# Writing the second half of a hidden tile behind an older chunk's matmuls, in a fused attention and expert kernel

## The chip, the cores and the metric

The kernel runs on one core of a Trainium2 chip. The metric is device microseconds of one execution; the time of a kernel is the median of its runs. The engines are named as in the profile: PE is TensorE (PEld its weight loads, which can run beside a matmul), DVE is VectorE, ACT is ScalarE, POOL is GpSimd, and SP issues the DMAs.

## The reference

```python
B, N, m, C = (4, 12480, 32, 128)
def mab(q, kv):
    s = scale * (q @ kv.transpose(0, 2, 1))
    a = np.exp(s - s.max(-1, keepdims=True))
    a /= a.sum(-1, keepdims=True) + 1e-09
    return a @ kv
h = mab(I, x)              # 32 inducing points look at all tokens
x = mab(x, h)              # each token looks at the 32 results
h = x @ w_in               # 49920 x 128 @ 128 x 2048
g = h * (1.0 / (1.0 + np.exp(-1.702 * h)))
out = g @ w_out            # 49920 x 2048 @ 2048 x 128
```

The four batches are 49,920 tokens in all. (The reference reuses the name `h`; the shortened lines above do too.)

## The kernel before, in words

The expert layer is nearly all of the work. Tokens go through it in blocks of 512 (96 whole blocks and 2 of 384 left over, `work`, lines 659 to 680). The hidden width of 2048 is cut into 16 chunks of 128, and two chunks make a group, so a block is 8 groups (`NG`) and the whole kernel has 784.

What is done for a group is in two functions.

`first(i)` (line 684) takes one PSUM tile `ph` of 128 x 2 x 512 from a pool of two (`ps_h`, line 98) and writes its two halves with one matmul each (line 693): the stacked attention weights `st` times `hw`, which is the second attention's values already multiplied by `w_in`. Then ScalarE reads both halves in one instruction and writes `g`, the activated values in fp32 (line 701). `hi`, the values rounded for the fast fp32 matmul, is made either by ScalarE from `ph` once more (line 705) or by DVE from `g` (line 707); `lo = g - hi` is made by DVE (line 708). Which engine makes `hi` is decided while the program is written out, by meters that add up an estimated cost for each instruction of ScalarE, DVE and TensorE (`Meter`, line 35; `act.t`, `dve.t`, `pe_.t` at lines 702 to 704). A `ph` tile is free again when ScalarE has read it for the last time.

`second(i, c)` (line 711) multiplies chunk `c` of group `i` by its part of `w_out` and adds it to the block's output in PSUM with three matmuls (`hi` by `wl`, `lo` by `wh`, `hi` by `wh`, lines 720 to 722). With the block's last chunk, ScalarE copies the output to SBUF (line 725) and the DMA to the output is put on a list, `stores`.

The order of all engines is written out by hand (`manual_schedule`, line 102), by the loop at lines 784 to 816. Each turn calls `first(i)`, puts the group's two chunks at the end of the list `under_way`, and then calls `second` for the oldest chunks until only `lag` are left (line 805). So in an ordinary turn TensorE gets two first products, side by side, and then six matmuls of two older chunks. `lag` starts at 6 chunks and grows by one every third turn up to 12 (`LAG`, `EXTRA`, line 813); a turn after which it has just grown leaves one chunk more in the list. The attention of the next batch is written in small steps behind each turn by the generator `rest` (line 809). When that generator yields `LUMP`, it has just put several exponentials into ScalarE's queue; then six older chunks are multiplied at once and `lag` falls back to 6 (lines 810 to 812). The list `stores` is issued on SP at the end of a turn (line 808), and `part`, a step of preparing `hw` for the next batch, is finished right behind `first(i)` (line 796).

Of the kernel before, what the change touches and what calls it, by code (L numbers as in the profile page):

```python
# [55 lines left out]
def set_attention_then_moe(ctx: ExitStack, tc, xT, x, indT, w_in, w_out, outT):  # L56
# [463 lines left out]
    def h_w_in(b, c):  # L520

        if b == 0:
            if c % 2 == 0:
                first_h.append(ps_h.tile([P, 2, 512], F32, tag="ph", name="ph"))
            pa = first_h[-1][:, c % 2]
        else:
            pa = ps_a.tile([P, 512], F32, tag="pa", name="pa")
        pe_.matmul(pa, hTs[b], w_in_sb[:, c * 512:(c + 1) * 512], start=True, stop=True)
        yield
        t = phw.tile([P, 512], F32R, tag="hw", name="hw")  # L530
        act.copy(t, pa)
        dve.tensor_sub(t[P // 2:P], pa[P // 2:P], t[P // 2:P].bitcast(F32))
        hw[b, c] = t
# [46 lines left out]
    def run(gen):  # L580
        for _ in gen:
            pass
# [101 lines left out]
    def first(i):  # L684
        bi, k = divmod(i, NG)
        key, of = work[bi]
        st = stacks[key]
        n = sum(p[2] for p in of)
        ph = ps_h.tile([P, 2, 512], F32, tag="ph", name="ph")
        for c in range(2):  # L690
            ch = 2 * k + c
            for b, at, w, _ in of:
                pe_.matmul(
                    ph[:, c, at:at + w], hw[b, ch // 4][:, ch % 4 * P:(ch % 4 + 1) * P],
                    st[:, at:at + w], start=True, stop=True,
                )
        hi = ph_.tile([P, 2, TOK], F32R, tag="hi", name="hi")
        lo = ph_.tile([P, 2, TOK], F32R, tag="lo", name="lo")
        g = pg.tile([P, 2, TOK], F32, tag="g", name="g")
        ph, hi, lo, g = ph[:, :, 0:n], hi[:, :, 0:n], lo[:, :, 0:n], g[:, :, 0:n]  # L700
        act.activation(g, ph, AF.Gelu_apprx_sigmoid)
        act.t = max(act.t, pe_.t)
        dve.t = max(dve.t, pe_.t)
        if act.t + 70 + 1.667 * n <= dve.t + 70 + 1.04 * n:
            act.activation(hi, ph, AF.Gelu_apprx_sigmoid)
        else:
            dve.tensor_copy(hi, g)
        dve.tensor_sub(lo, g, hi.bitcast(F32))
        parts[i] = hi, lo

    def second(i, c):
        bi, k = divmod(i, NG)
        key, of = work[bi]
        n = sum(p[2] for p in of)
        ch = 2 * k + c
        if ch == 0:
            outs[bi] = ps_o.tile([P, 512], F32, tag="po", name="pso")
        o = outs[bi][:, 0:n]
        hi, lo = parts.pop(i) if c else parts[i]
        pe_.matmul(o, wl[:, ch, :], hi[:, c, :], start=(ch == 0), stop=False)  # L720
        pe_.matmul(o, wh[:, ch, :], lo[:, c, :], start=False, stop=False)
        pe_.matmul(o, wh[:, ch, :], hi[:, c, :], start=False, stop=(ch == NCH - 1))
        if ch == NCH - 1:
            ob = po.tile([P, TOK], F32, tag="ob", name="ob")
            act.copy(ob[:, 0:n], o)
            for b, at, w, t0 in of:
                stores.append((i + 3, outT[:, t0:t0 + w], ob[:, at:at + w]))
            outs.pop(bi)
# [39 lines left out]
    under_way = []  # L768
# [7 lines left out]
    def lay_out():  # L776

        key = turns.pop(0)
        while key not in es:
            next(rest)  # L780
        return weights_of(*key), key

    i, lag, last = 0, LAG[0], 0
    while i < n or under_way:
        now[0] = i
        if i < n:
            if back is None and turns and i >= begin[turns[0]]:
                back, laid = lay_out()
            while back is not None and first_block[laid] * NG <= i:
                run(back)  # L790
                back = None
                if turns and first_block[turns[0]] * NG <= i:
                    back, laid = lay_out()
            first(i)
            if part is not None:
                run(part)
                part = None
            if products and products[0][0] == i:
                part = h_w_in(*products.pop(0)[1:])
                next(part)  # L800
            under_way += [(i, 0), (i, 1)]
            i += 1
        else:
            lag = 0
        while len(under_way) > lag:
            second(*under_way.pop(0))
        while stores and (stores[0][0] <= i or not under_way):
            nc.sync.dma_start(*stores.pop(0)[1:])
        if i < n and next(rest, None) is LUMP:
            while len(under_way) > LAG[0]:  # L810
                second(*under_way.pop(0))
            lag, last = LAG[0], i
        if lag < LAG[1] and i - last >= EXTRA:
            lag, last = lag + 1, i
        if back is not None and next(back, 0) == 0:
            back = None
# [33 lines left out]
```

## Time and profile before

| what | value |
|---|---|
| median of 3 runs | 1630.17 us (1630.16 to 1631.4) |
| the profiled execution's own time | 1632.7 us |
| its span, first to last instruction | 1630.9 us |
| mean granted clock of TensorE | 0.992 |
| first products (`ph<-st,hw`, 512 columns) | 1536, 401 ns each in the profile |
| matmuls into the output (`pso`, 512 columns) | 3 x 1536, 394 to 399 ns each |
| ACT `g<-ph` | 784, mean 1030 ns |
| ACT `hi<-ph` | 464, mean 1022 ns |
| DVE `hi<-g` | 320, mean 749 ns |
| DVE `lo<-g,hi` | 784, mean 1268 ns |
| ACT `ob<-pso` | 98, mean 591 ns |

A matmul's time in the profile includes its way through the array, which overlaps the next one; the distance between starts is what counts, not the duration. In a timeline a row gives the start, the duration, the engine, the line (46 for nearly all, a helper's), the operation, the tiles written and read, and how many instructions in a row were merged into it; in brackets stand the idle time of the engine ahead of it and what ended it. In the list of waits a row gives who waited, for whom, the total in us, the number of times and the longest. Releasers are inferred; "issue" means that the profile shows none.

### The profile page before, as it was taken

The numbers are of one execution on the slowest core, as the hardware profiler recorded it, in microseconds if no ns is written. First come the engines' busy times: TensorE is split into PE (matmuls) and PEld (weight loads), VectorE is DVE, ScalarE is ACT, GpSimd is POOL, SyncE is SP. The second block draws the span as 40 slices with busy tenths as digits, with TensorE's granted clock in tenths as the row PEclk, the third lists the DMA queues.
The fourth block names the chain that finished last, engine by engine and source line by source line (L and its number), as shares of the span: only waits on it lengthen the run. The fifth ranks groups of instructions, "written<-read, shape, count | busy, mean of one in ns | idle before, by whom it ended". The sixth has DMA issues, their size and how long they took to land.

```text
span 1630.9 us, 21863 instructions
## 1 busy us (share of the span) xinstructions
PE 1591.0 (98%) x7737; PEld 1233.0 (76%) x7737; DVE 1386.9 (85%) x1515; ACT 1331.5 (82%) x1513; POOL 197.9 (12%) x134
## 2 busy tenths in 40 slices
PE   6799999999999999999999999999999999999999
PEld 3477777787777877777766877777777888888887
DVE  7788978988889887888888988878988888889886
ACT  5488888888878878987888878988788888888885
POOL 4311100103101011011120110110121101101100
PEclk9899999999999999999999999999999999999999
DMA  8304219503042112850205101671301011011010
GB/s 338 104 16 175 64 37 203 120 19 97 19 142 76 43 39 56 184 126 20 91 14 202 40 27 39 136 183 40 97 16 42 25 39 46 20 39 46 22 44 20
DMA packets 81947, 126.66 MB, mean 78 GB/s; under 512 B 11632, under 2 KB 50096, under 8 KB 75696
## 3 DMA queue, kind: packets, MB, share of 16 engines
q1 hardware_dynamic: 81840, 125.26, 27.1%
q8 instruction: 63, 1.03, 0.3%
q14 instruction: 44, 0.36, 0.1%
HBM read 74.10 MB, written 25.56 MB: 61 GB/s over the span
## 4 chain that ended last, share of the span: by engine, by line
PE 88%; DVE 4%; ACT 3%; DMA 2%; issue 2%; SPq 1%; POOL 0%; ACTq 0%; DVEq 0%; POOLq 0%
PE pso L46 62%; PE ph L46 22%; PE pa L46 4%; DMA xt<-in_xT 2%; DVE lo L46 2%; ACT g L46 1%; ACT hi L46 1%; SPq L575 1%; DVE sm L46 1%; DVE hi L46 0%; DVE e L46 0%; DVE m L46 0%; DVE hw L46 0%; DVE t L46 0%; ACT s L46 0%
## 5 line engine op out<-in xcount | busy, mean ns | idle before, releaser
L46 DVE TENSOR_TENSOR lo<-g,hi 128x1024 fp32r<-128x1024 f32 (+1 forms) x784 | 983.1, 1268 | 134.4 <-ACT hi L46 122.0
L46 ACT ACTIVATE g<-ph 128x1024 f32<-128x1024 f32 (+1 forms) x784 | 804.3, 1030 | 232.2 <-PE ph L46 119.0
L46 PE MATMUL pso<-hi,wl 128*128 128x512 f32 (+1 forms) x1568 | 623.7, 398 | 0.0
L46 PE MATMUL pso<-hi,wh 128*128 128x512 f32 (+1 forms) x1568 | 617.3, 394 | 0.0
L46 PE MATMUL pso<-lo,wh 128*128 128x512 f32 (+1 forms) x1568 | 616.6, 393 | 0.0
L46 PE MATMUL ph<-st,hw 128*128 128x512 f32 x1536 | 491.2, 401 | 6.8 <-ACT hi L46 2.7
L46 ACT ACTIVATE hi<-ph 128x1024 fp32r<-128x1024 f32 (+1 forms) x464 | 474.1, 1022 | 0.0
L46 PEld LDWEIGHTS ph<-st,hw 128*128 128x128 f32 x1536 | 282.2, 188 | 100.5 <-issue 18.7
L46 PEld LDWEIGHTS pso<-lo,wh 128*128 128x128 f32 x1568 | 294.5, 188 | 73.2 <-issue 2.2
L46 PEld LDWEIGHTS pso<-hi,wl 128*128 128x128 f32 x1568 | 295.3, 188 | 70.4 <-issue 2.9
L46 PEld LDWEIGHTS pso<-hi,wh 128*128 128x128 f32 x1568 | 294.9, 188 | 70.3
L46 DVE CAST hi<-g 128x1024 fp32r<-128x1024 f32 x320 | 239.6, 749 | 77.0 <-ACT g L46 76.7
L547 POOL TENSOR_TENSOR e<-e,sm 128x512 f32<-128x512 f32 (+1 forms) x27 | 44.0, 1631 | 1132.8 <-DVE sm L46 1132.8
L46 ACT COPY ob<-pso 128x512 f32<-128x512 f32 (+1 forms) x98 | 58.0, 591 | 17.5 <-PE pso L46 17.5
L474 POOL TENSOR_TENSOR e<-e,m 128x512 f32<-128x512 f32 (+1 forms) x27 | 42.5, 1574 | 180.4 <-DVE m L46 135.8
L551 POOL TENSOR_TENSOR e<-e,ah 128x512 f32<-128x512 f32 (+1 forms) x27 | 49.5, 1834 | 2.2
L46 PE MATMUL pa<-xt,indT_sb 128*32 128x512 f32 x192 | 27.6, 676 | 17.2 <-DMA xt<-in_xT 17.2
L46 ACT ACT_TABLE_LOAD x28 | 35.9, 1283 | 9.8 <-issue 6.3
L550 POOL CAST ah<-e 128x512 fp32r<-128x512 f32 (+1 forms) x27 | 30.3, 1122 | 1.7
L46 PEld LDWEIGHTS pa<-xt,indT_sb 128*32 128x32 f32 x192 | 4.8, 114 | 28.7 <-issue 15.6
L46 PE MATMUL pa<-xt,hT 128*32 128x512 f32 x192 | 25.5, 637 | 1.0 <-DVE hT L46 1.0
L46 ACT ACTIVATE e<-e 128x512 f32<-128x512 f32 (+1 forms) x28 | 14.2, 572 | 9.5 <-DVE e L46 7.6
(97 smaller groups left out, 452.9 us busy)
## 6 DMA issues: line engine op xcount, KB each, us to landing
xt<-in_xT SPq DMA_DIRECT2D x48, 1024.0 KB, 7.1
out_T<-ob SPq DMA_DIRECT2D x96, 256.0 KB, 2.0
xn<-in_x SPq DMA_DIRECT2D x72, 256.0 KB, 6.8
st<-ahT SPq DMA_DIRECT2D x192, 64.0 KB, 2.0
st<-alT SPq DMA_DIRECT2D x192, 64.0 KB, 2.0
raw<-in_w_in SPq DMA_DIRECT2D x4, 512.0 KB, 8.6
raw<-in_w_out SPq DMA_DIRECT2D x4, 512.0 KB, 7.1
xt_last<-in_xT SPq DMA_DIRECT2D x4, 96.0 KB, 8.2
```

The source lines that it names most:

```text
L46: return f(*a, **k)
L474: eng.tensor_sub(e[0:q], e[0:q], m2[0:q, 0:k].unsqueeze(2).broadcast_to([q, k, M]))
L547: eng.tensor_mul(e[0:q], e[0:q], sm[0:q, 0:nb].unsqueeze(2).broadcast_to([q, nb, M]))
L550: eng.tensor_copy(ah[0:q, 0:w], e2[0:q])
L551: eng.tensor_sub(e2[0:q], e2[0:q], ah[0:q, 0:w].bitcast(F32))
L575: nc.sync.dma_start(st[32 * r:32 * r + 32, at:at + w].bitcast(F32), src[32 * j:32 * j + 32, 0:w])
```

## The change

`first` becomes a generator that stops once, between its two chunks. The loop writes the first chunk's product, then one older chunk's three matmuls if the list would be over `lag` with one more chunk in it, and then the rest of `first`: the second chunk's product, and all instructions of ScalarE and DVE. The number of older chunks multiplied in each turn does not change; one of them stands between the two products.

```diff
@@ -694,6 +694,8 @@
                     ph[:, c, at:at + w], hw[b, ch // 4][:, ch % 4 * P:(ch % 4 + 1) * P],
                     st[:, at:at + w], start=True, stop=True,
                 )
+            if c == 0:
+                yield
         hi = ph_.tile([P, 2, TOK], F32R, tag="hi", name="hi")
         lo = ph_.tile([P, 2, TOK], F32R, tag="lo", name="lo")
         g = pg.tile([P, 2, TOK], F32, tag="g", name="g")
@@ -791,7 +793,11 @@
                 back = None
                 if turns and first_block[turns[0]] * NG <= i:
                     back, laid = lay_out()
-            first(i)
+            begun = first(i)
+            next(begun)
+            if len(under_way) + 1 > lag:
+                second(*under_way.pop(0))
+            run(begun)
             if part is not None:
                 run(part)
                 part = None
```

## The prediction

> **What bounds the kernel now.** I read the page first: the span, the busy shares, and the chain that ended last.
>
> ```profile
> span 1630.9 us, 21863 instructions
> PE 1591.0 (98%) x7737; PEld 1233.0 (76%) x7737; DVE 1386.9 (85%) x1515; ACT 1331.5 (82%) x1513; POOL 197.9 (12%) x134
> PE 88%; DVE 4%; ACT 3%; DMA 2%; issue 2%; SPq 1%; POOL 0%; ACTq 0%; DVEq 0%; POOLq 0%
> ```
>
> TensorE sets the end. What it does not spend multiplying it spends waiting, and the change adds and removes no matmul. So the question is which waits of TensorE it makes or takes away. Next I read the groups by line, for what stands between a first product and the reuse of its PSUM tile, and the waits of TensorE's weight loads, since the semaphore wait of a first product sits on its load.
>
> ```profile
> L46 ACT ACTIVATE g<-ph 128x1024 f32<-128x1024 f32 (+1 forms) x784 | 804.3, 1030 | 232.2 <-PE ph L46 119.0 <-ACT g L46 81.7 <-DVE lo L46 16.2
> L46 ACT ACTIVATE hi<-ph 128x1024 fp32r<-128x1024 f32 (+1 forms) x464 | 474.1, 1022 | 0.0
> L46 ACT COPY ob<-pso 128x512 f32<-128x512 f32 (+1 forms) x98 | 58.0, 591 | 17.5 <-PE pso L46 17.5
> PEld ph L46 <- issue: 25.8, 46, 1.7
> PEld ph L46 <- ACT hi L46: 12.8, 25, 1.5
> PEld ph L46 <- ACT g L46: 4.5, 9, 1.7
> ```
>
> There are 784 groups. In 464 of them ScalarE reads the tile ph twice (g, then hi, about 1.95 us together, since the second starts 0.1 us before the first has ended), in the other 320 once. There are two ph tiles, so the first product of group i+2 waits until ScalarE has finished with group i. Today those waits are small: 43.1 us in 80 places, beside 784 groups. How much room is behind them is read from the timelines of an ordinary stretch: first TensorE, then ScalarE, then one weight load.
>
> ```profile
> 1458.27 0.63 PE L46 MATMUL ph<-st,hw 128*128 128x512 f32 x2
> 1460.14 0.63 PE L46 MATMUL ph<-st,hw 128*128 128x512 f32 x2
> 1463.87 0.39 PE L46 MATMUL ph<-st,hw 128*128 128x512 f32 x1
> ...
> 1460.85 1.03 ACT L46 ACTIVATE g<-ph 128x1024 f32<-128x1024 f32 x1 [0.87 <-ACT g L46]
> 1461.77 1.02 ACT L46 ACTIVATE hi<-ph 128x1024 fp32r<-128x1024 f32 x1
> ...
> 1463.64 0.42 PEld L46 LDWEIGHTS ph<-st,hw 128*128 128x128 f32 x2
> ```
>
> A group of eight matmuls takes 1460.14 - 1458.27 = 1.87 us, 0.233 us each. The pair of 1460.14 ends at 1460.77; g begins 0.08 later, hi ends at 1462.79, and the load that needs the tile starts at 1463.64: 0.85 us of room. ScalarE had been idle before that g, so here TensorE, not ScalarE, sets when the tile comes free.
>
> **The change part by part.** *The move in an ordinary group.* Three products of an older chunk go between the pair. ScalarE reads both halves at once, so g waits for the later one: 3 x 0.233 = 0.70 us later, while the first product of group i+2 is not later at all. The room falls from 0.85 to 0.15 us; a load can start 0.05 us after a release, so nothing waits. Cost: nothing, with 0.10 us of cover left. Where ScalarE is behind and g starts late anyway, the move is hidden by that lateness.
>
> *Groups with one chunk fewer.* The lag grows by one every third group from 6 to 12, after the start and after each of 13 lumps (four in each of three attentions, one in the first): 14 x 6 = 84 groups after which only one older chunk is multiplied. Before and after the change such a group has its pair side by side (the new condition is false in it), but the group ahead of it is split, and the load two groups on comes 0.70 us earlier than usual. One of them, in the timelines of TensorE, ScalarE and the loads:
>
> ```profile
> 1094.33 0.63 PE L46 MATMUL ph<-st,hw 128*128 128x512 f32 x2
> 1096.19 0.63 PE L46 MATMUL ph<-st,hw 128*128 128x512 f32 x2
> 1097.34 0.63 PE L46 MATMUL ph<-st,hw 128*128 128x512 f32 x2
> ...
> 1095.00 1.02 ACT L46 ACTIVATE g<-ph 128x1024 f32<-128x1024 f32 x1
> 1095.92 1.02 ACT L46 ACTIVATE hi<-ph 128x1024 fp32r<-128x1024 f32 x1
> ...
> 1097.11 0.42 PEld L46 LDWEIGHTS ph<-st,hw 128*128 128x128 f32 x2
> ```
>
> From 1096.19 to 1097.34 is only 1.15 us. hi of the group ahead ends at 1096.94 and the load starts at 1097.11: 0.17 us of room. With g 0.70 us later hi ends at 1097.64, and the load starts at 1097.69, 0.58 us late.
>
> What a late load costs is read from three pairs: one whose load had to wait a little, one where it waited long, and (above) 0.63 us for an undisturbed pair.
>
> ```profile
> 97.77 0.31 PEld L46 LDWEIGHTS ph<-st,hw 128*128 128x128 f32 x2 [0.15 <-ACT hi L46]
> 97.89 0.63 PE L46 MATMUL ph<-st,hw 128*128 128x512 f32 x2
> ...
> 1265.38 0.30 PEld L46 LDWEIGHTS ph<-st,hw 128*128 128x128 f32 x2 [0.30 <-ACT hi L46]
> 1265.38 0.73 PE L46 MATMUL ph<-st,hw 128*128 128x512 f32 x2
> ```
>
> A load normally leads its product by 0.23 us (1097.11 to 1097.34). At 97.77 the lead had shrunk to 0.12 and the pair still took 0.63. At 1265.38 it was gone and the pair took 0.73, since the next load was late too. So a load that is x late costs x - 0.23 + 0.10 = x - 0.13 us: for 0.58, 0.45 us. Where g starts 0.08 instead of 0.04 us behind its product (the two values above), it is 0.50.
>
> Going through the 84 in the timelines, 33 are of this kind: ScalarE makes hi of the group ahead, it is not already late, and no attention matmul stands in between. The first is the one at 97.77, the last the one at 1265.38. I take 0.48 for each: 33 x 0.48 = 15.8 us. In the others DVE makes hi (41% of groups), attention work delays the load, or ScalarE is late already. Bounds: if the 464/784 = 59% of hi groups held for all 84 with no shared cover, 50 x (0.58 + 0.10) = 34 us; the lower one is with the rivals.
>
> *Smaller losses behind these.* In 29 other places the room left now is below 0.70 us, because ScalarE has an output copy, an exponential or a table load in its queue, and there the delay comes through in part. The first and the last:
>
> ```profile
> 147.01 1.95 ACT L46 ACTIVATE g<-ph 128x1024 f32<-128x1024 f32 x2
> 148.51 0.42 PEld L46 LDWEIGHTS ph<-st,hw 128*128 128x128 f32 x2
> ...
> 1271.67 1.02 ACT L46 ACTIVATE hi<-ph 128x1024 fp32r<-128x1024 f32 x1
> 1273.24 0.42 PEld L46 LDWEIGHTS ph<-st,hw 128*128 128x128 f32 x2
> ```
>
> The load of 1273.24 has 0.55 us of room (hi ended at 1272.69), so it would be 0.20 late and cost 0.07 to 0.12; that of 148.51 has 0.47 (the first g ends at 148.04) and costs 0.14. At 0.15 each the 29 make 4.4 us. Bounds: 0 (TensorE, once delayed, leaves ScalarE time to catch up) and twice that.
>
> *The older chunk's other instructions.* An output copy follows the chunk that completes a block. While the lag is odd (9 groups in each of 14 ramps, 126 of 784, so 16 of the 98 copies) the completing chunk is the one moved, and its copy now stands ahead of g in ScalarE's queue. It can start when its product ends, 3 x 0.233 + 0.40 = 1.10 us after the group's start, takes 0.59, and g could start at about 1.38: 0.31 us late, behind 0.10 + 0.13 of cover where hi follows on ScalarE. 16 x 0.1, about 1 us; bounds 0 and 5. Its DMA to the output is only appended to a list at that point and is issued on SP at the end of the turn as before. Nothing is moved past another transfer or past POOL's queue.
>
> *The older products themselves.* The first of them needs hi and lo one matmul after the group's start, not two, and lo is up to 0.70 us later. DVE's lo is normally several groups ahead (the lag is 6 to 12 chunks, 3 to 6 groups of 1.87 us), except for the groups right behind a lump; 0 to 3 us, taken as none beyond what TensorE's own new waits cover.
>
> *The planner.* `first` reads TensorE's meter three products later, which raises ScalarE's and DVE's meters alike; who makes hi can change in or next to the 84 groups only, a cast of 0.75 us on one side against 1.02 on the other, off TensorE's path. Nothing, between -2 and 2.
>
> Sum: 15.8 + 4.4 + 1 = about 21 us. The execution profiled had a span of 1630.9 us; with it the sum is 1652, and against the median of the runs, 1630.2, it is **1651 us**.
>
> The Trainium skill's page "TensorE: Matmul & The Clock Gate", section "Back-to-back issue gap", gives about 216 ns for a warm matmul of 512 columns. The trace shows 233 here, and the measurement decides; by 216 the three products would delay g by 0.65 us, each of the 33 waits would be 0.05 shorter, and the sum 1.6 us less.
>
> **The rivals.** *The wait is hidden (no change).* If the products of older chunks that stand behind a waiting first product could start ahead of it, the 0.58 us would be filled and the time would be 1630. Against it: at 1265.38 above the load unit stood idle for 0.30 us with the loads of an older chunk's products two places further in its queue. The Trainium skill's same page, section "Step-by-step: what each phase is for", says that TensorE's queue pulls weight loads ahead of running matmuls but keeps the matmuls in program order. By its first half alone 1630 would come out; the idle 0.30 us agrees with the second half. The same time comes out if ScalarE's start is not tied to the second product as I read it.
>
> *The pair itself costs (faster).* The second product of a pair pays 0.10 us more when its load could not be made early, after a wait or after attention matmuls. That happens in 88 of the pairs; the loads of pso products seldom wait. If it is a cost of two first products side by side, and older products in between give time for that load, 88 x 0.10 = 8.8 us go: 1621. It decides only if the releases hold, that is, if fewer than some 18 of the waits of 0.48 appear. For it: the 0.73 row. Against it: a pso product also brings a load of its own, which would be just as late. If it came together with all 33 waits of 0.45 and none of the smaller losses, 15 - 9 = 6 us would be left: 1636, my lower bound.
>
> *The room is not there (much slower).* 0.15 us of room in the 464 hi groups is all that separates the ordinary group from a wait. If g starts 0.23 us later than I read (0.10 to the first late load, 0.13 of free lateness), every further 0.1 us costs 464 x 0.1 = 46 us: 1697. For it: ScalarE is busy 82%. Against it: the starts of g behind their products in the rows above spread over only 0.04 us (0.04 at 1095.00, 0.08 at 1460.85).
>
> **How the numbers follow.** The forecast has 0.80, the faster rival 0.07, the hidden wait 0.07, the vanished room 0.06. The range reaches from 1636 to the upper bounds, 34 + 9 + 2 = 45 us, 1675. Both rivals on the other side lie outside it. A measurement of this kernel can tell about 0.2% (3 us) from no change; the chances of that are faster 0.07, same 0.07, slower 0.86.
>
> **What would show it.** In the profile after: the waits of the ph loads for ScalarE's hi rise from 12.8 us to some 30, in some 30 more places; g's idle time for ph grows; ordinary stretches such as that at 1460 still take 1.87 us a group; the new waits stand two groups behind an end of three products instead of six. It is wrong if the ordinary groups lengthen (the third rival), if those waits don't grow (the first), or if the pairs of 0.73 turn into undisturbed products (the second).

## The result, and the profile after

The change makes the kernel slower by 0.5%: 1637.6 us median (1637.4 to 1639.0) against 1630.2 (1628.7 to 1631.4), ratio 1.0051 with a 95% interval of 1.0039 to 1.0063. The forecast was 1651 with a range from 1636 to 1675. The direction was right, the time lies just inside the range, and the size was three times too big: 7 us, not 21. Two executions among the experiments below ran in a slower state (1741.8 and 1951.0 us) and are left out of the ratios and the ranges.

First the page of the changed kernel (span, busy time, chain), and its groups that answer to those of before:

```profile
span 1637.2 us, 21856 instructions
PE 1594.2 (97%) x7737; PEld 1226.5 (75%) x7737; DVE 1389.4 (85%) x1518; ACT 1328.2 (81%) x1510; POOL 198.5 (12%) x134
PE 89%; ACT 4%; DVE 3%; issue 2%; DMA 2%; POOL 0%; SPq 0%; ACTq 0%; DVEq 0%; POOLq 0%
...
L46 ACT ACTIVATE g<-ph 128x1024 f32<-128x1024 f32 (+1 forms) x784 | 805.3, 1029 | 250.0 <-PE ph L46 131.1
L46 ACT ACTIVATE hi<-ph 128x1024 fp32r<-128x1024 f32 (+1 forms) x461 | 471.5, 1023 | 0.0
```

Busy times hardly move. Three `hi` have gone from ScalarE to DVE. The waits of TensorE's loads, from the list of waits of the changed kernel (who, for whom, total us, times, longest):

```profile
PEld ph L46 <- ACT hi L46: 41.2, 67, 1.5
...
PEld ph L46 <- issue: 16.1, 40, 1.7
...
PEld ph L46 <- ACT g L46: 7.4, 14, 1.4
PEld pa L46 <- DMA xt<-in_xT: 5.7, 3, 3.8
```

Loads that wait for ScalarE's `hi` went from 12.8 us in 25 places to 41.2 us in 67, more than the forecast's "some 30". The group that the prediction worked out by hand (the one followed by a pair at 1096.19 and one at 1097.34) stands here in the changed kernel, in the timelines of TensorE, ScalarE and the loads:

```profile
1100.90 0.39 PE L46 MATMUL ph<-st,hw 128*128 128x512 f32 x1
1101.82 0.39 PE L46 MATMUL ph<-st,hw 128*128 128x512 f32 x1
1102.76 0.63 PE L46 MATMUL ph<-st,hw 128*128 128x512 f32 x2
1104.26 0.50 PE L46 MATMUL ph<-st,hw 128*128 128x512 f32 x1 [0.18 <-ACT hi L46]
```
```profile
1102.26 1.03 ACT L46 ACTIVATE g<-ph 128x1024 f32<-128x1024 f32 x1
1103.18 1.02 ACT L46 ACTIVATE hi<-ph 128x1024 fp32r<-128x1024 f32 x1
```
```profile
1104.25 0.19 PEld L46 LDWEIGHTS ph<-st,hw 128*128 128x128 f32 x1 [0.60 <-ACT hi L46]
```

The split pair is 0.92 us apart. `hi` ends at 1104.20, the load starts 0.05 later, and the pair that took 1.15 us to come round before (1096.19 to 1097.34) takes 1.50 (1102.76 to 1104.26). A further 0.11 us is lost in the next turn, whose second load is late. That is 0.46 us, where the prediction had 0.45 to 0.50.

So the losses are there. To find the rest I set the start of every one of the 784 groups beside that of the kernel before, and looked at how the distance grows from turn to turn. In the two profiled executions:

| turns | us |
|---|---|
| 91 turns that became more than 0.04 us longer | +19.4 |
| turns 205 to 207, which wait for transfers of xT | -5.4 |
| five turns at groups whose `hi` is made by the other engine (191, 384, 385, 397, 583) | -3.2 |
| nine other turns that became shorter | -1.3 |
| the rest, about 675 turns, up to 0.04 us each | -4.1 |
| ahead of the first group | +0.9 |
| sum | +6.3 |

The spans differ by 1637.2 - 1630.9 = 6.3 us. The longer turns sum to nearly what was forecast. The forecast had none of the lines with a minus in its sum. Turn 397 could stand in the second line as well: TensorE waits for transfers of xT there too, and below the same microsecond is gained there once by the choice of engine alone and once by a delay alone.

### The profile page after: what moved, and what is told of

It reads as the page before. It is cut to its first block, busy times and chain, and to the rows that moved or that the text cites. A ratio compares the mean times of both kernels' runs of the same rounds, so it can differ in the third digit from the quotient of the medians.

```text
span 1637.2 us, 21856 instructions
## 1 busy us (share of the span) xinstructions
PE 1594.2 (97%) x7737; PEld 1226.5 (75%) x7737; DVE 1389.4 (85%) x1518; ACT 1328.2 (81%) x1510; POOL 198.5 (12%) x134
## 4 chain that ended last, share of the span: by engine, by line
PE 89%; ACT 4%; DVE 3%; issue 2%; DMA 2%; POOL 0%; SPq 0%; ACTq 0%; DVEq 0%; POOLq 0%
PE pso L46 62%; PE ph L46 22%; PE pa L46 5%; ACT hi L46 2%; DMA xt<-in_xT 2%; DVE lo L46 1%; ACT g L46 1%; DVE sm L46 0%; DVE hi L46 0%; DVE t L46 0%; DVE e L46 0%; ACT s L46 0%; DVE m L46 0%; POOL sq L595 0%; DVE hw L46 0%
## 5 line engine op out<-in xcount | busy, mean ns | idle before, releaser
L46 PE MATMUL ph<-st,hw 128*128 128x512 f32 x1536 | 604.1, 402 | 12.8 <-ACT hi L46 10.3
L46 PEld LDWEIGHTS ph<-st,hw 128*128 128x128 f32 x1536 | 286.5, 188 | 123.5 <-ACT hi L46 39.0
L46 DVE CAST hi<-g 128x1024 fp32r<-128x1024 f32 (+1 forms) x323 | 244.8, 758 | 71.0 <-ACT g L46 70.6
```

What stands on the lines that cost most here:

```text
L46: return f(*a, **k)
```

## The experiments

In all of these the ratio is to the kernel before in runs on the same chip; its median was between 1629.4 and 1633.3 us, by the chip.

**The choice of engine for hi, put back.** The meters are read as if the older chunk had not been moved.

```diff
+            ahead[0] = pe_.t
             if len(under_way) + 1 > lag:
                 second(*under_way.pop(0))
+            ahead[0] = pe_.t - ahead[0]
...
-        act.t = max(act.t, pe_.t)
-        dve.t = max(dve.t, pe_.t)
+        act.t = max(act.t, pe_.t - ahead[0])
+        dve.t = max(dve.t, pe_.t - ahead[0])
```

> The change, but the meters are read as if the older chunk had not been moved, so that the engine of hi is chosen as in the kernel before (464 on ScalarE). Theory A: of the 33 places that the prediction counted, those that vanished because hi had changed engines come back: waits for hi 3 to 6 us above the change's, 1639 to 1644. Theory B (the choice makes the new time): 1626 to 1630.

Measured: ratio 1.0069 (1.0057 to 1.0082), 1644.3 us. `hi` is on its engine of before in 776 of the 784 groups. Loads wait 42.7 us for it, only 1.5 above the change, where 3 to 6 were expected. Turns longer by over 0.04 us sum to 22.4 us; all of the 33 turns that the prediction had picked from the trace of before are among those that lose 0.25 us or more, and only six others are. The 33 and the turn behind each lose 15.3 us, where the prediction had 15.8. In the change itself 30 of the 33 are; in the other three `hi` had moved to DVE.

**That choice alone**, in the order of the kernel before:

```diff
+            ahead[0] = 0
+            if len(under_way) + 1 > lag:
+                ahead[0] = 3 * sum(p[2] for p in work[under_way[0][0] // NG][1]) / 2.4
             first(i)
...
-        act.t = max(act.t, pe_.t)
-        dve.t = max(dve.t, pe_.t)
+        act.t = max(act.t, pe_.t + ahead[0])
+        dve.t = max(dve.t, pe_.t + ahead[0])
```

> The order of the kernel before, with the choice of engine for hi that the change brings (three fewer on ScalarE, some hundred exchanged with a neighbour). Theory A: 1630 within 2. Theory B: 1636 to 1638.

Measured: 0.9983 (0.9975 to 0.9992), 2.8 us faster. The five turns of the table become 2.8 us shorter here as well. The two ratios multiply to 1.0052, the change's own 1.0051 (1.0040 in a second run, below): what the change does by moving matmuls costs 0.7%, and a by-product, the planner's other choice, gives 0.17% back.

**Both first products together, behind one older chunk.**

```diff
+            if len(under_way) + 1 > lag:
+                second(*under_way.pop(0))
             first(i)
```

> One older chunk, then both first products side by side, then the second older chunk; choice of engine as before. Theory A: both halves move together, so the room from a release to the next load is that of the kernel before: no new waits, 1630 within 2. Theory C' (what costs is that g and the chain behind it come 0.70 us later against the older chunks): waits as in the change, 1637. What the ordinary turns take (1.853 or 1.867 us) tells whether two first products side by side are what made some turns of the kernel before 13 ns longer.

Measured: 1.0007 (0.9998 to 1.0016); loads wait 13.5 us for `hi`, in 24 places. `g` comes just as late against the older chunks as in the change, and it costs nothing that the runs can tell. What costs is the distance from the pair's first product, which must wait for the tile, to its second, which releases `g`.

**Twice the distance.** Both older chunks stand between the products.

```diff
-            if len(under_way) + 1 > lag:
+            while len(under_way) + 2 > lag and under_way:
                 second(*under_way.pop(0))
```

> Both older chunks stand between the first products, so g comes 1.40 us later instead of 0.70; choice of engine read as before. Theory A: the room of an ordinary hi group, 0.85 us, is overdrawn by 0.55; loads are 0.60 late in nearly each of the 464 hi groups and cost about 0.37 to 0.47 each: 160 to 220 us more, 1790 to 1850. If the cost of the change were one per turn with a split (about 700 of them) and not tied to the room, twice the distance would give at most twice the change's cost, 1650.

Measured: 1791.7 us, ratio 1.0997 (1.0976 to 1.1018), 162 us slower, from two runs. In the list of waits of this kernel:

```profile
PEld ph L46 <- ACT hi L46: 225.0, 344, 1.7
```

The time lies at the lower edge of what theory A gave, with waits in 344 places rather than in nearly all of the 464. The loss is some fourteen times that of one chunk with the choice of engine held (11 us), for twice the distance. It is no price per split but an overdrawn room: with one chunk between, an ordinary group keeps about 0.1 us; with two it is short by half a microsecond. A place late in this kernel shows it, the second product of one group and the first of the next, with 0.43 us of idle TensorE between them:

```profile
1606.13 0.40 PE L46 MATMUL ph<-st,hw 128*128 128x512 f32 x1
1606.96 0.50 PE L46 MATMUL ph<-st,hw 128*128 128x512 f32 x1 [0.43 <-ACT hi L46]
```

**No split right ahead of a short turn.** Choice of engine as before.

```diff
-            if len(under_way) + 1 > lag:
+            short_next = lag < LAG[1] and i + 1 - last >= EXTRA
+            if len(under_way) + 1 > lag and not short_next:
                 second(*under_way.pop(0))
```

> The pair is split as in the change, except in the turns whose next turn is one chunk short (there it stays side by side); the choice of engine for hi is that of the kernel before. Theory A (the new time is waits of the ph loads behind a split group ahead of a short turn; apart from them ordinary turns became 13 ns shorter): the waits for hi fall back to about 13 us of loads as before, ordinary turns stay at 1.853 us, and the time is 1626, between 1624 and 1629, below both kernels. Theory B (the new time comes from another choice of engine for hi): 1630. Theory C (splitting costs in every group): 1636 to 1638, since 90% of the splits are still there.

Measured: 1.0029 (1.0018 to 1.0040), 1638.0 us. My theory failed here: half of the waits stayed (28.2 us, 52 places). One of them, in the timelines of TensorE and ScalarE:

```profile
292.50 0.50 PE L46 MATMUL ph<-st,hw 128*128 128x512 f32 x1
293.54 0.39 PE L46 MATMUL ph<-st,hw 128*128 128x512 f32 x1
294.47 0.63 PE L46 MATMUL ph<-st,hw 128*128 128x512 f32 x2
296.33 0.63 PE L46 MATMUL ph<-st,hw 128*128 128x512 f32 x2
297.80 0.50 PE L46 MATMUL ph<-st,hw 128*128 128x512 f32 x1
```
```profile
293.97 1.03 ACT L46 ACTIVATE g<-ph 128x1024 f32<-128x1024 f32 x1 [0.84 <-PE ph L46]
294.89 1.02 ACT L46 ACTIVATE hi<-ph 128x1024 fp32r<-128x1024 f32 x1
295.79 1.03 ACT L46 ACTIVATE g<-ph 128x1024 f32<-128x1024 f32 x1
296.69 1.05 ACT L46 ACTIVATE hi<-ph 128x1024 fp32r<-128x1024 f32 x1
```

The group of 294.47, right ahead of the short turn, is whole, and its pair is done at 295.10. But `g` starts only at 295.79: ScalarE is still busy with the group of 292.50, which is split, and whose `g` began late, at 293.97. From one `g` to the next ScalarE takes 1.82 us here (293.97 to 295.79; the next `g` starts 0.1 us before `hi` has ended), in a turn of 1.86 (294.47 to 296.33). So it makes up some 0.04 us of its lateness in a turn and carries the rest along. (The expectation of the next run puts the 1.95 us from the start of `g` to the end of `hi` beside the 1.86; that is not what a group costs ScalarE.) The load that needs the tile waits until 297.79.

**A split only while the lag is 12**, so in none of the growing turns; ScalarE's instructions are exactly in the order of the kernel before.

```diff
-            if len(under_way) + 1 > lag:
+            if lag == LAG[1] and len(under_way) + 1 > lag:
                 second(*under_way.pop(0))
```

> The pair is split only while the lag stands at 12, so in none of the turns in which it grows; choice of engine as before, and all instructions of ScalarE in the order of the kernel before. Theory A', which the split-unless-short run asks for (a split group leaves ScalarE 0.70 us later, and ScalarE, which needs 1.95 us for g and hi in turns of 1.86, carries that lateness into the short turn even when the group right ahead of it is not split): with no split in the growing turns the waits for hi fall back to some 13 us, ordinary turns are 1.853 us, and the time is 3 to 5 us below the kernel before, ratio 0.997 to 0.998. If splitting costs in ordinary groups too, the ratio is 1.000 or above.

> The kernel of e6 again: 0.998 to 0.999 if the shorter turns are worth 2 us or more in the median, 1.000 if not.

Measured: 1.0000 (0.9990 to 1.0010) and, on another chip, 0.9997 (0.9986 to 1.0007). The waits for `hi` fell back (17.0 and 16.4 us, where the kernel before has 12.8), and longer turns sum to 1.9 us where the change has 19.4. So the cost of the change sits in the growing turns, as predicted, and the split costs nothing that the runs can tell in ordinary ones. The gain that I expected from shorter ordinary turns did not show in the runs; more on this below.

**The lag grows only behind a group whose hi is DVE's**, in the change and in the kernel before:

```diff
-        if lag < LAG[1] and i - last >= EXTRA:
+        if lag < LAG[1] and i - last >= EXTRA and early[0]:
```

(`early[0]` is set to False or True where `hi` goes to ScalarE or DVE.)

> The change, but the lag grows only in a turn whose group has hi made by DVE, so that the group ahead of a short turn releases its tile 0.95 us earlier. Theory A': fewer of the new waits, waits for hi 15 to 25 us of loads instead of 41, time 1628 to 1634 where the kernel before has 1630 to 1633. If lateness carried over from the hi group one turn earlier decides, it stays near the change's 1637.

> The kernel before with the same rule for growing the lag and no split. Theory A': only the waits that the kernel before has at short turns (some 15 places of 0.1 to 0.5 us) go: 0 to 4 us below it.

Measured: with the split 1.0002 (0.9993 to 1.0010), without it 0.9980 (0.9971 to 0.9988); loads wait 14.7 and 10.9 us for `hi`. One condition on when turns may be short brings the change back to the time of the kernel before, with 707 of the 784 pairs still split: most of the loss needs a short turn behind a late release. Not all of it: beside the same rule without the split, on the same chip, the split still costs 2.7 us (1629.2 against 1626.5), and its loads wait longer for `g` too (8.0 us against 1.4). The rule also changes the engine of `hi` in some 300 groups, which these two runs do not hold fixed.

**A delay of TensorE alone.** If the waits are all there, something gives time back. Spare matmuls were put into the kernel before, in one place, and then in another:

```diff
+            if i == 196:
+                t = ps_a.tile([P, 512], F32, tag="pa", name="spare")
+                for _ in range(60):
+                    nc.tensor.matmul(t[:, 0:P], ident, ident, start=True, stop=True)
             first(i)
```

> The kernel before, and 60 spare matmuls of 128 columns (about 0.111 us each, 6.7 us) on TensorE alone, ahead of turn 196, some 9 turns before TensorE waits for transfers of xT. Theory A (a delay of TensorE ahead of that place is partly given back there, which took 5 us off the change's own delays): 3 to 5 us of the 6.7 come back, the kernel is 1.5 to 4 us slower than before. Rival (nothing is given back, the change's waits were fewer than the trace seems to show): 6 to 7 us slower.

> The same 60 spare matmuls ahead of turn 640, where no transfer is waited for afterwards: 6.5 to 7.5 us slower than before by both theories; it gives the size of the delay.

The spare matmuls took twice what I had reckoned, 13.3 us (each fp32 product ran as two matmuls, 120 in the profile), so the numbers expected are to be doubled. Measured: 1.0058 (1.0043 to 1.0072), 9.4 us, at turn 196, and 1.0075 (1.0061 to 1.0088), 12.2 us, at turn 640. The intervals overlap, so the totals alone do not settle it. The one profile of each does: of the 13.3 us, turns 205 to 207 give back 4.9 and turn 397 another 1.1; behind turn 640 no turn gives any back. The place is seen in the timelines of SP, which issues the transfers, and of TensorE; first the kernel before:

```profile
474.44 2.30 SPq L166 DMA_DIRECT2D xt<-in_xT  x4
...
479.41 1.07 PE L46 MATMUL pa<-xt,indT_sb 128*32 128x512 f32 x8 [0.56 <-DMA xt<-in_xT]
483.24 1.94 PE L46 MATMUL pa<-xt,indT_sb 128*32 128x512 f32 x8 [2.77 <-DMA xt<-in_xT]
```

the kernel with the early delay:

```profile
488.30 2.15 SPq L166 DMA_DIRECT2D xt<-in_xT  x4
...
493.44 1.07 PE L46 MATMUL pa<-xt,indT_sb 128*32 128x512 f32 x8
495.73 1.07 PE L46 MATMUL pa<-xt,indT_sb 128*32 128x512 f32 x8 [1.22 <-DMA xt<-in_xT]
```

and the change:

```profile
481.06 2.29 SPq L166 DMA_DIRECT2D xt<-in_xT  x4
...
487.07 1.07 PE L46 MATMUL pa<-xt,indT_sb 128*32 128x512 f32 x8
488.75 1.07 PE L46 MATMUL pa<-xt,indT_sb 128*32 128x512 f32 x8 [0.61 <-DMA xt<-in_xT]
```

A TensorE that arrives later loses less here, for two reasons. The first is idle time: 0.56 and 2.77 us before, 1.22 with the early delay, 0.61 in the change. The transfers are issued later too (6.6 us in the change, where TensorE comes to turn 205 8.2 us later, and 13.9 with the delay, where it comes 14.7 later), but not quite as late as TensorE, and the second lands sooner: its matmuls start 8.80 us after the first issue before, 7.43 with the delay, 7.69 in the change. Why it lands sooner was not found. The second reason is the clock. Three stretches, before, with the early delay and in the change (PE busy, the other engines, and near the end the granted clock):

```profile
482.50:489.00 6.50, 5.76 (x19) 3.71 (x20) 0.66 (x1) 2.40 (x3) 0.00 (x0) 0.50 0.56 236
```
```profile
487.00:502.00 15.00, 13.78 (x73) 10.33 (x72) 10.93 (x14) 12.21 (x15) 0.00 (x0) 1.00 0.82 311
```
```profile
482.00:492.00 10.00, 8.80 (x49) 6.03 (x49) 7.36 (x9) 7.06 (x9) 0.00 (x0) 1.00 0.98 389
```

Before, TensorE ran at a granted clock of 0.50 behind its wait; in the other two the clock stayed at 1.00. At 0.50 the second row's eight matmuls took 1.94 us instead of 1.07, and turns 206 and 207 took 1.33 and 0.55 us longer than in the change. So of the 5.4 us that come back in the change, about 2.7 are idle time and 2.7 a slow stretch of the clock that no longer happens. The second profile of the change (below) shows the same 5.4 us and the same clock of 1.00. The Trainium skill's page "TensorE: Matmul & The Clock Gate", Part 1, says that the clock is at half speed after an idle window of about 3.4 us; the 0.50 agrees, but the longest idle time ahead of it here was shorter, 2.77 us.

**The change again, and a version that beats both.** The change was run once more, on another chip. The fastest parts were then put together: the order of the kernel before, the lag growing behind DVE's `hi`, and the change's reading of the meters (the three edits shown above); then the same with the pair split while the lag is 12.

> The change itself once more, on the chip of the following runs: ratio 1.004 to 1.006, waits of the ph loads for hi some 41 us, ordinary turns 1.853 us.

> The order of the kernel before, the lag growing only behind a group whose hi is DVE's, and the meters read as in the change: both parts that were faster alone. Theory A: they remove different waits, so the ratios multiply, 0.996. If both remove the same waits: 0.998.

> The kernel of e13 again, side by side with e14 on one chip: ratio 0.995 to 0.997.

> The kernel of e13 (lag grows behind DVE's hi, choice as in the change) with the pair split while the lag is 12; ScalarE's order is that of e13. If the shorter ordinary turns of the profiles are there in all runs: 1 to 4 us below e13, by the number of 1.867 us turns that e13 has. If they come and go from run to run in kernels without a split, half of that or nothing that can be measured.

Measured: the change 1.0040 (1.0027 to 1.0053); the version without a split 0.9960 (0.9946 to 0.9973) and, again, 0.9972 (0.9963 to 0.9981); with the split at full lag 0.9971 (0.9960 to 0.9982), beside the latter. Whether the two gains add is not settled. The first run fits the product of the two ratios, 0.9963; the second lies between that and the lag rule alone (0.9980), and its interval holds both. The profiles show no sum: the lag rule alone has a span of 1625.1 us, the two together 1625.0 and 1624.8, though the waits for `hi` are shorter (8.1 us against 10.9). The lag rule alone already makes turns 191 and 583 1.1 us shorter each, and those are two of the five turns that the choice of engine had shortened. The split adds nothing to either.

## Why the prediction was right or wrong

*What bounds the kernel; which wait decides.* Right. Pair together, split, split wider: the cost follows the room between a release and the next load. (Of the 43.1 us in 80 places that the prediction read as waits for ScalarE, 25.8 in 46 are "issue", waits for which the profile shows nobody; ScalarE's are 17.3 us in 34.)

*The ordinary group.* "Nothing waits" was right, with the 0.10 us of cover it stated: the split at full lag brings only a few more waits for `hi` (17.0 us against 12.8) and no time that can be measured, and twice the distance costs 162 us, at the lower edge of 160 to 220.

*The 84 groups.* Right in place and price: 33 of 33 places with the choice of engine held, 0.46 us for the one worked out by hand, 15.3 us for all 33 against 15.8. What the prediction missed is that the lateness is inherited: a group two turns ahead of the short one is enough, which the first experiment on this showed.

*The sum.* This is the step that failed. It added what TensorE loses, 15.8 + 4.4 + 1, and took the total as the kernel's. The losses came out at 19.4 us, or 22.4 with the choice held, where it had 21. Three things were set at nothing, or not at all:

- Time given back. No term was there for it, though the trace of before held 8.3 us of loads and more of matmuls waiting for xT. 5.4 us of the change's delay disappeared at one such place, and 4.8 with the choice held: about half of it less waiting, the other half a stretch at half clock that follows the long wait of before and not the shorter one. The delay put in by hand shows the same in the same turns.
- The planner, "nothing, between -2 and 2". It was worth -2.8 us by itself and also removed three of the 33 waits. The prediction let the engine of `hi` change in or next to the 84 groups only; it changed in 109 groups.
- Ordinary turns, "nothing". In the two profiles they are 4.1 us shorter.

With -5.4, -3.2 and -1.3, 19.4 becomes 9.5 us; with the 4.1 it is 5.4. The runs gave 7.4.

*The range.* That 1637.6 lies inside it is luck. The lower bound, 1636, was worked out from the rival in which the pair itself costs; the time came down to it by other ways, which the prediction did not have.

*The rivals.* The vanished room did not happen. The hidden wait did not either: behind each late load the older products stood still. The pair that itself costs was not borne out either: a product behind a late load loses its 0.11 us as a `pso` just as it did as a `ph`.

*What stays open.* Whether the shorter ordinary turns are worth anything. The two runs of the split at full lag say at most 0.14%, and the version with the fewest waits is no faster with the split than without. On one chip the kernel before spreads more (1624.6 to 1632.4 us in 27 runs, the split at full lag 1627.0 to 1630.6 in the 10 beside it); on another the two spread alike (1625.8 to 1631.7 and 1624.9 to 1630.8). Part of that spread goes with the clock: on the first of these chips the 14 runs of the kernel before with a mean granted clock of 0.994 or more average 1628.6 us, the 8 with 0.992 or less 1631.6. How often its runs have the short turns, no run here tells.

## What to carry to other kernels

When a producer's tile is waited for as a whole, the time from its first write to its last is taken from the room of the buffer ring; ask for the tightest turn of the schedule, not the usual one, and let lateness pass from one group to the next on the engine that releases. When the losses are found, ask which later wait for something else (a transfer above all) will swallow part of them, and whether a shorter wait there keeps the clock up: only what is left behind the last such wait reaches the end. And if an order is written out by a planner, moving a line moves its decisions too; hold them fixed in one run, and change them alone in another.

## What the runs showed of the hardware that was not expected

Turns of eight matmuls of 512 columns, with nothing waited for, come in two lengths, 1.853 and 1.867 us (231.7 and 233.3 ns a matmul). In the profiles before and after, no two neighbouring turns differ: a stretch keeps one length until TensorE is next interrupted. In the profile before 285 turns are of the long kind and 255 of the short; in the change 1 and 496. With the pair split the long kind hardly appears (1 to 23 turns in the splits of one chunk), with the pair side by side it makes up 79 to 285, also behind an older chunk (282). Late in the changed kernel, the first products of four turns in a row, 1.85 us apart:

```profile
1469.44 0.39 PE L46 MATMUL ph<-st,hw 128*128 128x512 f32 x1
1471.29 0.39 PE L46 MATMUL ph<-st,hw 128*128 128x512 f32 x1
1473.14 0.39 PE L46 MATMUL ph<-st,hw 128*128 128x512 f32 x1
1475.00 0.39 PE L46 MATMUL ph<-st,hw 128*128 128x512 f32 x1
```

What sets the length at an interruption was not found.

The stretch at half clock near 482 us stands in 12 of the 17 profiles, for 3.4 or 6.8 us. It is missing in the five in which TensorE comes to turn 205 6.8 us later or more than in the kernel before; in the 12 it comes at most 3.8 us later.
